# Issuing half of a kernel's input loads from GpSimd instead of SyncE

## The chip, the cores and the metric

The kernel runs on one core of a Trainium2 chip. The metric is device time in microseconds (us); lower is better. Most runs of the kernel before agree within 0.5% (10 of the 11 of the first job lie within 0.5% of their median, 274.85 us). A run is called fast or slow by its distance from the fastest run of the same kernel (over 1.5% is slow). Ratios are computed as the mean time of one kernel's fast runs over that of the other's of the same rounds, so they are not quite the ratio of the medians that are quoted beside them.

TensorE is called PE, VectorE DVE, ScalarE ACT, GpSimd POOL and SyncE SP, as in the profile. PEld is PE's weight load. A name with q (SPq, POOLq) is the engine's sequencer issuing a DMA. The profile counts the DMAs of every engine on the same 16 DMA engines. In it, q1 is SyncE's queue, q10 ACT's (both "hardware_dynamic") and q0 is GpSimd's ("software_dynamic").

## The reference

Linear attention with cosine weights, then an MLP mixer over tokens and channels, eight batches, all in fp32 at the boundary:

```python
# q, k, v: (8 batches, 8 heads, 576 rows, 64); weights: 576x256, 256x576, 512x1536, 1536x512
phi(x) = concat(relu(x) * cos, relu(x) * sin)      # 64 -> 128 features, angle grows with the row
kv  = einsum('bhsf,bhsd->bhfd', phi(k), v);  z = phi(k).sum(rows)
x   = (phi(q) @ kv) / (phi(q) @ z + 1e-6)           # heads joined: (8, 576, 512)
h   = relu(x.T @ w_tok1) @ w_tok2
u   = x + h.T
out = u + relu(u @ w_ch1) @ w_ch2                   # ... cut
```

## The kernel before

It is a pipeline over batches, written as one order of instructions. While PE works on the channel MLP of batch p, it also does the attention and the token MLP of p+1, the features of p+2 are made on ACT and DVE, and the inputs of p+3 are loaded. The first part (batches 0 and 1, and the loads up to batch 4) follows a list of words, PLAN; the rest is a loop over channel blocks with hooks in numbered slots.

Three kinds of DMA matter here. Loads bring q, k and v in rows of 1024 or 1280 bytes. Transposes turn a bf16 tile inside SBUF; `qpT` (features of q) and `uT` (input of the channel MLP) are read by PE as weights and operands. Stores write the result. All of these go out from SyncE, so one queue (q1, 48.77 MB in the page below) holds them, in program order in SyncE's timeline below. GpSimd loads the weights early, and later only casts.

```python
def load(b, t, hs=slice(0, H), eng=nc.sync):          # two DMAs: 512 rows of 1024 B, 512 rows of 1280 B
    ...
    for par in (1 - b % 2, b % 2):
        n, f = count(b % 2, par), row0(b % 2, par)
        dmas.append(eng.dma_start(out=x[par::2, hs, raw_span(b % 2, par)], in_=...))

def ldp(b, t, g, g_="n"):                             # as ld, but issued by GpSimd; unused before
    d = load(b, t, heads(g), nc.gpsimd)
...
    def turnx(self, j, n):                            # qpT: 16 + 16 + 8 blocks of 128x128 a batch
        nc.sync.dma_start_transpose(out=self.sb("qpT")[:, j * H:(j + n) * H, :], in_=self.qp[:, j:j + n]...)
    def ubc(self, g, eng="P"):                        # ub: bf16 cast of u on GpSimd
        copy(eng, self.sb("ub")[:, js, :], self.u[:, js, :])
    def utx(self, g):                                 # uT: two transposes of 256 KB a batch
        nc.sync.dma_start_transpose(out=self.sb("uT")[:, 2*g:2*g+2]..., in_=self.ub[:, 2*g:2*g+2]...)
    def o(self, j):                                   # stores; store_batch does the same in the loop
        ...nc.sync.dma_start(out=out_rows(self.b, p_, j - 1, 2), in_=self.u[p_::2, j - 1:j + 1, :])
...
def hooks_for(n, m, nxt):                             # n = p+1, m = p+2, nxt = p+3; at(slot, function, ...)
    if nxt is not None:
        at(0, load, nxt, "k")
        at(0, load, nxt, "q")
        at(9, load, nxt, "v")
    ...                                               # kv, num (reads qpT), mix, u_all (casts ub, uT)
    if m is not None:
        ...                                           # v casts on GpSimd in slots 3 to 7
        at(12, m.turnx, 0, 2)
        at(15, m.turnx, 2, 2)
        at(16, m.turnx, 4, 1)
```

## Time and profile before

| | before |
|---|---|
| time, median of 3 runs | 275.25 us (274.46 to 275.7) |
| span of the profiled run | 273.6 us |
| PE busy | 262.1 us, 96% |
| PE's waits for transposes | 1.6 us, once |
| channel blocks, start to start | 27.6, 29.3, 27.6, 27.6 us |

The first lines are of the page of the kernel before: the span, each engine's busy time with its share of the span and its instructions; each DMA queue's packets, megabytes and share of the 16 engines' time; and the chain of work that ended last, summed by engine.

```profile
span 273.6 us, 4855 instructions
PE 262.1 (96%) x1923; PEld 137.7 (50%) x1941; DVE 172.1 (63%) x346; ACT 110.9 (41%) x176; POOL 47.6 (17%) x67
...
q1 hardware_dynamic: 74512, 48.77, 66.0%
q0 software_dynamic: 4144, 3.77, 9.1%
...
PE 89%; DMA 5%; DVE 4%; issue 1%; DVEq 0%
```

PE is the bound, and there is little else to gain. The one wait inside the pipeline shows in the same chain, in order of time (start, length, what):

```profile
117.84 5.79 DMA qpT<-qp
...
123.68 0.43 PE nf L390 x8
```

The chain passes through 5.79 us of a qpT transpose, but PE had other work during most of it: it waited 1.6 us. What it costs is read better from the starts of the kv matmuls, one set for each channel block, in PE's timeline (start, length, engine, line, operation):

```profile
89.11 1.44 PE L361 MATMUL kv<-vbf,kp 128*128 128x65 bf16 x40
116.71 1.43 PE L361 MATMUL kv<-vbf,kp 128*128 128x65 bf16 x40
146.04 1.43 PE L361 MATMUL kv<-vbf,kp 128*128 128x65 bf16 x40
```

The distances are 27.60 and 29.33 us, and the next ones are 27.6 us again: the block with the wait is 1.7 us longer. SyncE's timeline shows why the transpose came late (start, length of the issue, sequencer, line, operation):

```profile
83.08 2.63 SPq L472 DMA_TRANSPOSE uT<-ub  x2
...
100.67 4.38 SPq L143 DMA_DIRECT2D vt<-in_v_dram  x2
105.94 6.82 SPq L472 DMA_TRANSPOSE uT<-ub  x2
112.85 1.22 SPq L503 DMA_TRANSPOSE uT_tail<-utb  x1
114.17 1.59 SPq L354 DMA_TRANSPOSE qpT<-qp  x1
```

The uT transposes of 105.94 us stand behind loads that the DMA engines have not finished: the first of the v loads of 100.67 us landed 10.7 us after its issue. The transposes' own issue takes 6.82 us instead of 2.63, and the qpT transposes behind them are late. The uT transposes of 83.08 us, by contrast, had the engines nearly to themselves: all 2268 packets of the stretch were under 512 B. The view of the DMAs between 83 and 86 us gives the queue's packets, megabytes and share of the 16 engines' time, and for each kind of issue its count and median time to landing in us:

```profile
q1 hardware_dynamic: 2268, 0.56, 98.4%
...
uT<-ub SPq DMA_TRANSPOSE x2, 3.2
```

### The profile page before, as it was taken

Reading aid. Unit: us, or ns where it says so; the run is one execution under the profiler, and the core shown is the slowest. Engines: PE = TensorE matmul, PEld = TensorE weight load, DVE = VectorE, ACT = ScalarE, POOL = GpSimd, SP = SyncE. Lnnn points to the kernel's source line nnn. Section 1 sums busy time; section 2 is a strip of 40 time slices with the busy share of each in tenths; the row PEclk is TensorE's granted clock in tenths of the full one; section 3 lists DMA queues with packets and bytes.
Section 4 is the critical chain, followed back from the end, with each engine's and each line's share of the span. In section 5 each row is a group of like instructions: output and inputs, shape, how many; then the busy total and the mean of one; then the engine's idle time right before and its main releaser. Section 6 shows DMA issues by size and latency. Waiting matters only on the chain.

```text
span 273.6 us, 4855 instructions
## 1 busy us (share of the span) xinstructions
PE 262.1 (96%) x1923; PEld 137.7 (50%) x1941; DVE 172.1 (63%) x346; ACT 110.9 (41%) x176; POOL 47.6 (17%) x67
## 2 busy tenths in 40 slices
PE   6988999999999999989999999999999999999994
PEld 2875556465444644454446544554455444444443
DVE  6489798899872658835794769476837643424422
ACT  2885281475590548052903391339133201301300
POOL 2172070040041043400250026002000120000000
PEclk9999999999999999999999999999999999999998
DMA  6999999999999999999999948900980062012012
GB/s 206 360 238 170 287 199 238 365 207 211 378 249 196 330 380 361 206 216 297 340 196 235 352 156 175 230 37 2 219 204 2 0 153 98 0 44 109 2 67 87
DMA packets 79079, 53.37 MB, mean 195 GB/s; under 512 B 47824, under 2 KB 76496, under 8 KB 79056
## 3 DMA queue, kind: packets, MB, share of 16 engines
q1 hardware_dynamic: 74512, 48.77, 66.0%
q0 software_dynamic: 4144, 3.77, 9.1%
q10 hardware_dynamic: 400, 0.52, 0.5%
q8 instruction: 15, 0.25, 0.4%
q14 instruction: 8, 0.07, 0.1%
HBM read 35.85 MB, written 9.44 MB: 166 GB/s over the span
## 4 chain that ended last, share of the span: by engine, by line
PE 89%; DMA 5%; DVE 4%; issue 1%; DVEq 0%
PE o_ps L606 25%; PE c_ps L589 25%; PE c L512 8%; PE o L524 7%; PE b L433 6%; PE u L460 5%; PE kv L361 4%; DMA kt<-in_k_dram 3%; PE nf L390 3%; DMA qpT<-qp 2%; DVE kp L332 1%; PE ut L488 1%; PE tr L345 1%; PE o_ps L598 1%; PE nm L390 1%; DVE x L413 1%
## 5 line engine op out<-in xcount | busy, mean ns | idle before, releaser
L268 ACT ACTIVATE h<-c_ps 128x512 bf16<-128x512 f32 x52 | 31.0, 597 | 109.6 <-PE c_ps L589 66.0
L606 PE MATMUL o_ps<-wc,h 128*128 128x512 bf16 x317 | 71.5, 379 | 0.4
L589 PE MATMUL c_ps<-uT,wc 128*128 128x512 bf16 x288 | 70.4, 379 | 0.0
L606 PEld LDWEIGHTS <-h 128*128 128x128 bf16 x324 | 31.7, 98 | 38.2
L589 PEld LDWEIGHTS <-wc 128*128 128x128 bf16 x336 | 30.8, 98 | 32.6
L270 DVE TENSOR_SCALAR h<-c_ps 128x512 bf16<-128x512 f32 x32 | 22.0, 688 | 28.4 <-PE c_ps L589 28.4
L264 POOL CAST ub<-u 128x1024 bf16<-128x1024 f32 x14 | 14.9, 1066 | 106.4 <-issue 63.2
L330 ACT ACTIVATE qp<-qt,cos_t 128x512 bf16<-128x512 f32 x33 | 23.1, 713 | 13.6 <-DMA qt<-in_q_dram 12.1
L609 DVE TENSOR_TENSOR u<-o_ps,u 128x512 f32<-128x512 f32 x24 | 16.5, 689 | 18.5 <-PE o_ps L606 18.5
L264 POOL CAST vbf<-vt 128x512 bf16<-128x512 f32 (+3 forms) x28 | 19.5, 731 | 49.6 <-DMA vt<-in_v_dram 47.3
L512 PE MATMUL c<-uT,wc 128*128 128x512 bf16 x96 | 22.7, 379 | 0.1
L524 PE MATMUL o<-wc,h 128*128 128x512 bf16 x92 | 21.6, 379 | 0.2
L413 DVE TENSOR_TENSOR x<-nf,den 128x512 bf16<-128x512 f32 x30 | 20.7, 692 | 1.0
L330 ACT ACTIVATE qp<-qt,sin_t 128x512 bf16<-128x512 f32 x30 | 21.1, 712 | 0.0
L390 PEld LDWEIGHTS <-qpT 128*128 128x128 bf16 x320 | 15.2, 98 | 11.6 <-DMA qpT<-qp 2.1
L332 DVE TENSOR_SCALAR kp<-kt,cos_t 128x512 bf16<-128x512 f32 x30 | 17.4, 582 | 5.1 <-DMA kt<-in_k_dram 5.1
L465 DVE TENSOR_TENSOR u<-u,x 128x1024 f32<-128x1024 f32 x16 | 19.4, 1220 | 1.7 <-PE u L460 1.7
L433 PE MATMUL b<-x,w 128*128 128x512 bf16 (+1 forms) x84 | 19.8, 354 | 0.3
L332 DVE TENSOR_SCALAR kp<-kt,sin_t 128x512 bf16<-128x512 f32 x31 | 17.9, 582 | 0.6 <-DMA kt<-in_k_dram 0.6
L409 DVE TENSOR_SCALAR den<-nf 128x8 f32<-128x8 f32 x30 | 5.0, 166 | 17.7 <-PE nf L390 17.7
L460 PE MATMUL u<-B,w 128*128 128x512 bf16 x64 | 16.1, 379 | 0.0
L524 PEld LDWEIGHTS <-h 128*128 128x128 bf16 x96 | 9.1, 98 | 10.2
(92 smaller groups left out, 249.4 us busy)
## 6 DMA issues: line engine op xcount, KB each, us to landing
out_dram<-u SPq DMA_DIRECT2D x32, 256.0 KB, 2.7
qt<-in_q_dram SPq DMA_DIRECT2D x8, 640.0 KB, 7.4
kt<-in_k_dram SPq DMA_DIRECT2D x8, 640.0 KB, 7.8
qt<-in_q_dram SPq DMA_DIRECT2D x8, 512.0 KB, 6.3
kt<-in_k_dram SPq DMA_DIRECT2D x8, 512.0 KB, 6.7
vt<-in_v_dram SPq DMA_DIRECT2D x6, 640.0 KB, 9.9
vt<-in_v_dram SPq DMA_DIRECT2D x6, 512.0 KB, 8.8
wc<-in_moe_w_ch_dram POOLq DMA_DIRECT2D x4, 384.0 KB, 7.7
```

Source lines behind the costliest of these rows:

```text
L264: (nc.scalar.copy if eng == "A" else ENG[eng].tensor_copy)(dst, src)
L268: nc.scalar.activation(dst, src, AF.Relu)
L330: nc.scalar.activation(dst, src, AF.Relu, scale=tab)
L332: ENG[eng].tensor_scalar(dst, src, scalar1=tab, scalar2=0.0, op0=ALU.mult, op1=ALU.max)
L390: nc.tensor.matmul(nm[:, hh * (D + 1):(hh + 1) * (D + 1)], self.qpT[:, j * H + h, :], self.kv[:, h, :D + 1], start=(not eps or hh == 0), s ...
L413: nc.vector.tensor_mul(dst, nmv[:, :, :, :D], den_b)
L433: nc.tensor.matmul(b1[:, mi], w1[:, col(self.c, j), mi * P:(mi + 1) * P], self.x[:, j, cs], start=(j == 0 and (g == 2 or mi == 0)), stop=( ...
L460: nc.tensor.matmul(ps[:, jj], w2[:, ki, 1 + 2 * g + jj, :], self.B1[:, ki, :], start=(ki == 0), stop=(ki == NT - 1))
L512: nc.tensor.matmul(ps, wc1[:, ki, mi * P:(mi + 1) * P], self.uT[:, :, ki, :], start=(ki == 0), stop=(ki == NCC - 1))
L524: nc.tensor.matmul(self.ps["o", j], self.h1[:, ki, j * P:(j + 1) * P], wc2[:, ki, :], start=(ki == 0), stop=(ki == NCH - 1))
L589: nc.tensor.matmul(c_ps, wc1[:, ki, mi * P:(mi + 1) * P], uT[:, :, ki, :], start=(ki == 0), stop=(ki == NCC - 1))
L606: nc.tensor.matmul(o_ps, h1[:, ki, j * P:(j + 1) * P], wc2[:, ki, :], start=(ki == 0), stop=(ki == NCH - 1))
```

## The change

The intent is to take the loads of batches 4 to 7 out of the transposes' queue. Loads go to GpSimd, and SyncE's queue holds only transposes and stores from then on, so that no transpose stands behind a load.

```diff
-utx.2.1 dnj.1.0.0 utx.2.0 ld.4.q.2 dnj.1.2.0 tb.1 ...
-... cast.3.2.1.2.P feat.3.k.2.2.1.D ld.4.v.2.k22 dnj.1.1.0 dnj.1.1.1 ld.4.k.2.k32 ...
+utx.2.1 dnj.1.0.0 utx.2.0 ldp.4.q.2 dnj.1.2.0 tb.1 ...
+... cast.3.2.1.2.P feat.3.k.2.2.1.D ldp.4.v.2.k22 dnj.1.1.0 dnj.1.1.1 ldp.4.k.2.k32 ...
@@ hooks_for
         if nxt is not None:
-            at(0, load, nxt, "k")
-            at(0, load, nxt, "q")
-            at(9, load, nxt, "v")
+            at(0, load, nxt, "k", slice(0, H), nc.gpsimd)
+            at(0, load, nxt, "q", slice(0, H), nc.gpsimd)
+            at(9, load, nxt, "v", slice(0, H), nc.gpsimd)
```

More of the change, by code (lines that the diff above doesn't have):

```diff
@@ L52 @@
 cast.3.1.1.2.P uo.2.1 ubc.2.1 uo.2.0 dnj.1.3.0 dnj.1.3.1 cast.3.3.1.2.D turnx.3.0.2 feat.3.k.0.2.0.A ubc.2.0
-utx.2.1 dnj.1.0.0 utx.2.0 ld.4.q.2 dnj.1.2.0 tb.1 feat.3.k.4.2.0.A dnj.1.2.1 cast.3.0.1.2.D o.1.2
-feat.3.k.1.2.0.A cast.3.2.1.2.P feat.3.k.2.2.1.D ld.4.v.2.k22 dnj.1.1.0 dnj.1.1.1 ld.4.k.2.k32 feat.3.k.3.2.1.A
-dnj.1.0.1 feat.3.k.3.2.0.A feat.3.k.1.2.1.A o.1.0 o.1.3 tm.2 to.2 o.1.1
+utx.2.1 dnj.1.0.0 utx.2.0 ldp.4.q.2 dnj.1.2.0 tb.1 feat.3.k.4.2.0.A dnj.1.2.1 cast.3.0.1.2.D o.1.2
+feat.3.k.1.2.0.A cast.3.2.1.2.P feat.3.k.2.2.1.D ldp.4.v.2.k22 dnj.1.1.0 dnj.1.1.1 ldp.4.k.2.k32
+feat.3.k.3.2.1.A dnj.1.0.1 feat.3.k.3.2.0.A feat.3.k.1.2.1.A o.1.0 o.1.3 tm.2 to.2 o.1.1
 """
```

## The prediction

> **What bounds the kernel now.** TensorE: the page gives PE 262.1 us busy of a 273.6 us span (96%), granted clock near 1.00; the chain of waits is 89% PE, 5% DMA, 4% DVE. Its DMA part is 7.8 us for the first k load (untouched) and one wait of 5.79 us on a transpose of q features (qpT), 117.84 to 123.68 us. That wait costs less than its length: channel blocks start at 88.4, 116.0, 145.3, 172.9, 200.5 us and last 27.6 us, but the one with this wait 29.3 us. So 1.75 us is all that faster transposes can win; elsewhere PE is busy 1.95 to 2.00 of every 2 us (table of windows).
>
> **Why that wait is there.** In the SyncE queue's timeline, loads of batches 4 and 5 are issued from 85.8 to 105 us, at 311 to 393 GB/s. The uT transposes behind them take 3.97 and 2.76 us to issue (1.26 undisturbed) and 7.9 and 5.3 us to land (3.1 to 3.3), and push the qpT transposes from about 110 to 114.2 and 117.8 us.
>
> **What the change moves.** 24 load issues go from SyncE (0.6 to 0.75 us each, more when backed up) to GpSimd, which paid 0.7 to 0.8 us per weight load: 17 to 19 us more on an engine 17% busy. Order on PE, DVE and ACT is the same. GpSimd's queue is in order, so a load's wait for its buffer holds back later casts; I find no harmful case: the k loads wait for the last k feature (115.3 us) with only v casts behind them, due 30 us later, and the ub casts come after loads already issued.
>
> **Where it helps.** [...] Then transposes no longer stand behind whole loads: batch 4's qpT goes out near 110 and 113 us and lands before its use at 122. Gain: 1.75 us, likely the whole.
>
> **Where it hurts.** Loads start as soon as GpSimd is free: q4 near 82.2 instead of 85.8 us, v4 near 85 instead of 88.6, k5 near 88 instead of 95. The uT transposes of batch 2 (issued 83.08 and 84.4, landed near 87.5, first read by PE at 88.4: 0.9 us of slack) had the DMA engines almost alone; now they share them with a stream of loads. If they take 5 to 7 us to land instead of 3.2, PE stalls 1 to 3 us; my estimate is 1.6. Later, k of batches 6 and 7 (near 115 and 145 us) overlaps the last qpT transposes, which have 2 to 5 us of slack: 0.2 us.
>
> **Sum.** 275.25 - 1.75 + 1.6 + 0.2 = about 275.2; predicted 275.2 us, 8 in 10 between 273.2 and 278.2. Faster by over 2%: 0.01; within 2%: 0.94; slower by over 2%: 0.05.
>
> **What the profile would show.** Right: the block near 116 us lasts 27.6 us and its qpT wait is gone; a new PE wait on a uT transpose near 88 us; SyncE issues of uT back to 1.3 us in the next block; 14 MB more on the software queue; GpSimd issues near 0.75 us. Wrong: PE waits for qpT or uT at 145 us or later; ub casts starting later after DVE's u.
>
> **What would make it wrong.** The share that transposes get against loads is unmeasured: if small, several transposes stall PE by 3 us or more each; if large, the stall at 88 us vanishes (273.5). GpSimd issue may take much longer for 512 rows of 1 to 1.25 KB, or block when many loads are outstanding, delaying ub casts.

## The result, and the profile after

| | before | after |
|---|---|---|
| median, first job | 274.86 us (274.15 to 275.7, 4 runs) | 324.02 us (320.94 to 329.42, 4 runs) |
| ratio of fast runs | | 1.1698 [1.1624, 1.1773] |

The kernel became 17% slower. Two of the four runs count as slow by the rule above, the profiled one among them. The changed kernel was therefore run again (the first experiment, below): 327.37 us, ratio 1.1927, with a profile in the fast state. That profile is the one read here. The scatter of about 3% belongs to the changed kernel.

The page of the changed kernel, same lines as before:

```profile
span 323.1 us, 4860 instructions
PE 267.5 (83%) x1923; PEld 139.7 (43%) x1941; DVE 170.0 (53%) x346; ACT 111.0 (34%) x176; POOL 62.9 (19%) x91
...
q1 hardware_dynamic: 61840, 34.61, 44.4%
q0 software_dynamic: 7600, 17.93, 24.2%
...
PE 59%; DMA 30%; DVE 3%; SPq 3%; POOL 2%; issue 1%; ACT 0%; POOLq 0%; DVEq 0%
```

PE is busy 83% of the time and the chain is 30% DMA. PE's waits (engine, line, what for: total, times, longest):

```profile
PE nf L390 <- DMA qpT<-qp: 25.6, 2, 15.5
PE c_ps L589 <- DMA uT<-ub: 20.0, 1, 20.0
```

And their places in PE's timeline, with the wait in brackets:

```profile
109.63 1.87 PE L589 MATMUL c_ps<-uT,wc 128*128 128x512 bf16 x4 [19.98 <-DMA uT<-ub]
160.46 0.62 PE L390 MATMUL nf<-kv,qpT 128*128 128x65 bf16 x8 [15.53 <-DMA qpT<-qp]
202.18 0.62 PE L390 MATMUL nf<-kv,qpT 128*128 128x65 bf16 x8 [10.05 <-DMA qpT<-qp]
```

Three waits on transposes hold nearly the whole loss. The span is 323.1 - 273.6 = 49.5 us longer. The waits are 45.6 us, less the 1.6 us that were there before. PE's busy time is 267.5 - 262.1 = 5.4 us more. That sums to 49.4 us. The extra busy time has a visible source: four matmuls of this shape took 1.87 us at 109.63 us, and 1.03 us at 88.25 us in the kernel before. The table by stretches gives the granted clock there (stretch, its length, busy time of PE, PEld, DVE, ACT and POOL, clock, DMA share, GB/s):

```profile
104.00:106.00 2.00, 0.00 (x0) 0.00 (x0) 0.00 (x0) 0.00 (x0) 0.00 (x0) 0.50 1.05 355
110.00:112.00 2.00, 2.00 (x17) 1.17 (x16) 0.00 (x0) 0.42 (x1) 0.00 (x0) 0.50 1.01 324
```

The clock is at 0.50 while PE idles and still 0.50 in the first 2 us of work after the wait; at 114 us it is back at 1.00. The stretches at 0.50 behind the two qpT waits end at 164.0 and 205.0 us. PE was busy 9.5 us in the three together; if that work takes half the time at a clock of 1.00, as an estimate 4.7 of the 5.4 us come from the clock (the four matmuls above took 1.87 against 1.03 us). Here a long wait is paid a second time.

Now the DMAs. The second of the two uT transposes, issued at 85.65 us, in the view of the DMAs from 86 to 88 us:

```profile
uT<-ub SPq DMA_TRANSPOSE x1, 23.8
```

It took 23.8 us to land instead of 3.2 (the first, issued at 84.27 us, took 10.2). What the engines did meanwhile, from 96 to 106 us (packets, MB, share of the 16 engines' time):

```profile
DMA packets 1646, 3.51 MB, mean 351 GB/s; under 512 B 930, under 2 KB 930, under 8 KB 1645
...
q0 software_dynamic: 804, 3.28, 93.2%
q1 hardware_dynamic: 841, 0.21, 10.6%
```

This is the central reading. The two queues sent almost the same number of packets, 804 and 841. But a packet of the loads holds 4096 or 5120 B (by the record of each packet in the first profile of this kernel), and a packet of the transposes 0.21 MB / 841 = 256 B. Packet for packet, the transposes get one part in ten of the engines' time (10.6%). Nothing is idle in this stretch: the two shares add up to 103.8%, and the engines move 351 GB/s. The transposes, on which PE waits, get 6% of the bytes.

The page itself shows the packets' size. SyncE's queue lost 74512 - 61840 = 12672 packets and GpSimd's gained 7600 - 4144 = 3456, for the same 14.16 MB in 24 loads. That is 528 packets a load from SyncE and 144 from GpSimd. A load has 512 rows: 512 + 16 and 128 + 16, with 16 more packets per load in either case, of 4 B by the same record. SyncE sends one row in a packet, GpSimd four.

The rest of the change did what it was meant to. GpSimd's timeline in that stretch:

```profile
83.35 1.43 POOL L143 DMA_DIRECT2D qt<-in_q_dram  x2
...
86.25 1.38 POOL L143 DMA_DIRECT2D vt<-in_v_dram  x2 [0.30 <-POOL vbf L264]
87.61 2.74 POOL L143 DMA_DIRECT2D kt<-in_k_dram  x4
```

An issue takes about 0.7 us, loads go out earlier than before (v of batch 4 at 86.25 instead of 88.57 us, k of batch 5 by 90 instead of 95), and the uT transposes of the next block, with no loads about, take 2.96 us for two issues, not 6.82.

### The profile page after: what moved, and what is told of

It is laid out like the page before. It is cut to its first block, busy times and chain, and to the rows that moved or that the text cites. A ratio compares the mean times of both kernels' runs of the same rounds, so it can differ in the third digit from the quotient of the medians.

```text
span 327.6 us, 4878 instructions
## 1 busy us (share of the span) xinstructions
PE 269.3 (82%) x1941; PEld 140.2 (43%) x1941; DVE 170.4 (52%) x346; ACT 111.0 (34%) x176; POOL 63.0 (19%) x91
## 3 DMA queue, kind: packets, MB, share of 16 engines
q1 hardware_dynamic: 61840, 34.61, 45.0%
## 4 chain that ended last, share of the span: by engine, by line
PE 65%; DMA 25%; DVE 5%; SPq 2%; POOL 1%; issue 1%; DVEq 0%; POOLq 0%
PE c_ps L589 20%; PE o_ps L606 19%; DMA qpT<-qp 13%; DMA uT<-ub 8%; PE b L433 5%; PE c L512 4%; PE u L460 4%; PE o L524 3%; PE kv L361 3%; DMA kt<-in_k_dram 2%; PE nf L390 2%; DMA out_dram<-u 2%; DVE kp L332 1%; PE tr L345 1%; PE ut L488 1%; SPq L354 1%
## 5 line engine op out<-in xcount | busy, mean ns | idle before, releaser
L589 PE MATMUL c_ps<-uT,wc 128*128 128x512 bf16 x288 | 74.3, 394 | 23.6 <-DMA uT<-ub 23.6
L589 PEld LDWEIGHTS <-wc 128*128 128x128 bf16 x336 | 31.6, 100 | 58.5 <-issue 27.8
L606 PEld LDWEIGHTS <-h 128*128 128x128 bf16 x324 | 31.7, 98 | 38.2
L264 POOL CAST ub<-u 128x1024 bf16<-128x1024 f32 x14 | 14.9, 1068 | 138.1 <-DVE u L465 118.2
L390 PE MATMUL nf<-kv,qpT 128*128 128x65 bf16 x240 | 13.2, 199 | 26.2 <-DMA qpT<-qp 25.8
L330 ACT ACTIVATE qp<-qt,cos_t 128x512 bf16<-128x512 f32 x33 | 23.1, 713 | 15.5 <-DMA qt<-in_q_dram 13.5
L264 POOL CAST vbf<-vt 128x512 bf16<-128x512 f32 (+3 forms) x28 | 18.4, 694 | 40.5 <-DMA vt<-in_v_dram 39.3
L413 DVE TENSOR_TENSOR x<-nf,den 128x512 bf16<-128x512 f32 x30 | 20.7, 692 | 1.0
L433 PE MATMUL b<-x,w 128*128 128x512 bf16 (+1 forms) x90 | 21.2, 368 | 0.0
L332 DVE TENSOR_SCALAR kp<-kt,cos_t 128x512 bf16<-128x512 f32 x30 | 16.4, 549 | 4.7 <-DMA kt<-in_k_dram 4.7
L332 DVE TENSOR_SCALAR kp<-kt,sin_t 128x512 bf16<-128x512 f32 x31 | 16.8, 548 | 0.9 <-DMA kt<-in_k_dram 0.9
```

The lines of the kernel that those rows point to most:

```text
L264: (nc.scalar.copy if eng == "A" else ENG[eng].tensor_copy)(dst, src)
L330: nc.scalar.activation(dst, src, AF.Relu, scale=tab)
L332: ENG[eng].tensor_scalar(dst, src, scalar1=tab, scalar2=0.0, op0=ALU.mult, op1=ALU.max)
L390: nc.tensor.matmul(nm[:, hh * (D + 1):(hh + 1) * (D + 1)], self.qpT[:, j * H + h, :], self.kv[:, h, :D + 1], start=(not eps or hh == 0), s ...
L433: nc.tensor.matmul(b1[:, mi], w1[:, col(self.c, j), mi * P:(mi + 1) * P], self.x[:, j, cs], start=(j == 0 and (g == 2 or mi == 0)), stop=( ...
L589: nc.tensor.matmul(c_ps, wc1[:, ki, mi * P:(mi + 1) * P], uT[:, :, ki, :], start=(ki == 0), stop=(ki == NCC - 1))
```

## The experiments

Theories of why the transposes are slow, conjectures of the author's that the runs tell apart below:

1. Shares: each DMA engine takes a packet from each queue in turn, whatever its size, so what counts is the size of the packets beside the transposes.
2. Switching: mixing two queues, or transposes with copies, costs the DMA engines time, so all traffic slows.
3. Transposes as such are sensitive, and a plain copy of the same packets would not be.
4. GpSimd as such: its queue is favoured, or its load issues hold back its own casts in order, and transposes start late.

Where an expectation uses letters, S1 is the first of these, S2 the second and S3 the first half of the fourth; S alone says only that transposes starve beside GpSimd's loads. Other letters are explained where they stand. The experiments e1 to e4 ran in one job, e5 to e8 in a second, e9 to e11 in a third, and e12 alone; each job had its own runs of the kernel before (medians 274.85, 274.68, 275.38 and 275.51 us). Kernels called wrong give wrong output and are used for their traces.

### e1: the changed kernel again

No edit.

> The changed kernel itself, once more, for a profile in the fast state. Every theory: about 320 to 323 us, PE waits of some 15 to 24 us on a uT transpose near 88 us and on qpT transposes of the next two channel blocks, in a fast run too. If the long waits show only in slow runs, the slow state and not the change makes them.

Measured: 327.37 us (324.93 to 329.31), ratio 1.1927 [1.1866, 1.1988]. The profile is the one read above. The result stands, in a second job and in fast runs alone, though above the 320 to 323 us expected. Theory 4's second half falls here: GpSimd's first ub cast of batch 2 starts 1.9 us after DVE's u (2.0 before), and the first uT transpose is issued at 84.27 us, as soon as SyncE has issued the qpT transposes ahead of it, again as before.

### e2: only batch 4's loads moved

```diff
-            at(0, load, nxt, "k", slice(0, H), nc.gpsimd)
-            at(0, load, nxt, "q", slice(0, H), nc.gpsimd)
-            at(9, load, nxt, "v", slice(0, H), nc.gpsimd)
+            at(0, load, nxt, "k")
+            at(0, load, nxt, "q")
+            at(9, load, nxt, "v")
```

> Only batch 4's loads (the three words of the schedule list) are issued by GpSimd; batches 5 to 7 stay on SyncE. Theory S (transposes starve while GpSimd-issued loads are outstanding): the uT transposes of batch 2 land only when most of 3.5 MB of q4, v4, k4 have been moved, near 97 to 100 us instead of 87.5, so PE stalls about 10 us at 88 us, and later blocks are as before: about 285 us. Rival G (GpSimd's in-order queue delays its casts): ub casts would start late after DVE's u and the loss would not go with transposes; with only 6 loads moved and none of them waiting long, about 276 us.

Measured: 292.01 us (290.17 to 293.21), ratio 1.0612 [1.0565, 1.0659]. PE waits 18.3 us for uT, and for no qpT. The second uT transpose, issued at 83.32 us, took 22.8 us to land. So the first wait comes from moving six load issues alone, and the two qpT waits from the other eighteen. But the wait is nearly twice the 10 us expected of 3.5 MB of loads, and the time is 7 us over; e8 comes back to this.

### e6: only the loads of batches 5 to 7 moved

The reverse of e2: PLAN as before, the three hooks as in the change.

> The other half of the change: batch 4's loads stay on SyncE, those of batches 5 to 7 are issued by GpSimd. Theory S1: the wait of 20 us at 88 us is gone or small (k5 and q5 are issued near 89 us, after the uT transposes), the two later waits on qpT of 10 to 17 us each stay: 298 to 305 us. Together with batch 4's part (292.0) the two losses should add up to about that of the whole change, 17 + 25 to 30 = 42 to 50 us. Rival (one cause early on that shifts everything): the later waits go with the first one, under 285 us.

Measured: 306.15 us median, and only one of four runs counts as fast (299.72; the others 305.41, 306.9, 310.28), so no ratio is given, and the profile is a slow one. It shows two qpT waits, 18.7 us together, and one of 6.7 us on a DVE add that itself waited for a store. Added up, e2 loses 17 us and the fast run of e6 25 us, 42 together, against 46 to 52 for the whole change. The parts nearly add up; the scatter of the runs hides the rest.

### e3: the changed kernel, with q and k loads held back until the transposes have landed

The q load of batch 4 waits for the last uT transpose of batch 2, and the k load of each later block waits for the last qpT transpose of the batch before. All 24 loads stay on GpSimd.

```diff
-utx.2.1 dnj.1.0.0 utx.2.0 ldp.4.q.2 dnj.1.2.0 tb.1 ...
+utx.2.1 dnj.1.0.0 utx.2.0 ldp.4.q.2.uT2 dnj.1.2.0 tb.1 ...
...
+    def gated(b, t, name):
+        gate(load(b, t, slice(0, H), nc.gpsimd)[0], name)      # wait for landed[name]
...
-            at(0, load, nxt, "k", slice(0, H), nc.gpsimd)
+            at(0, gated, nxt, "k", f"qpT{nxt - 2}")
```

> All 24 loads still issued by GpSimd, but batch 4's q waits for the last uT transpose of batch 2 to land, and the k load at the start of each channel block waits for the last qpT transpose of the batch before it, so that few transposes are in flight with these loads. Theory S: the starving goes, 273 to 277 us. Rival G (in-order GpSimd queue): GpSimd waits longer than before, so at least as slow as the changed kernel, 320 us or more. Rival D (GpSimd-issued loads are slow in themselves): still 290 us or more, with PE, ACT or DVE waiting for q, k or v loads.

Measured: 275.47 us (274.71 to 276.33), ratio 1.0022 [0.9993, 1.0051]. The same loads on the same queue, moved in time by a few microseconds, cost nothing: the whole 17 to 19% is the overlap in time with transposes. One wait on a transpose was left:

```profile
125.09 0.43 PE L390 MATMUL nf<-kv,qpT 128*128 128x65 bf16 x8 [2.96 <-DMA qpT<-qp]
```

Here the v load of batch 5, which has no gate, goes out at 102.09 us and meets the uT transposes of 105.92 us.

### e4: the disputed share measured by itself

A small kernel (wrong) in phases. Each phase issues 4.2 MB of loads, then two 512 KB transposes (or plain SBUF copies in 256 B rows) from SyncE. Phases differ in who issues the loads, and in their row length in words of 4 bytes.

```python
def loads(tag, eng, words):        # two loads of 2 MB, rows of `words` fp32, not adjacent in memory
    src = flat.rearrange("(p a f) -> p a f", p=P, f=words * 9 // 8)
    ... eng.dma_start(out=t, in_=src[:, i * n:(i + 1) * n, :words])
PHASES = (("A", None, 0, "t"), ("B", "g", 256, ""), ("C", "g", 256, "t"), ("D", "a", 256, ""), ("E", "a", 256, "t"),
          ("F", "a", 1024, "t"), ("G", "g", 1024, "t"), ("H", None, 0, "c"), ("I", "g", 256, "c"), ("J", "a", 256, "c"),
          ("K", "s", 256, "t"), ("L", "a", 64, "t"))     # g GpSimd, a ACT, s SyncE; t transposes, c copies
```

> A kernel made for measuring (its result is wrong on purpose: it stores zeros). Twelve phases one after the other: A two transposes of 512 KB on SyncE alone; B 4.2 MB of loads in 1 KB rows from GpSimd alone; C B with the transposes; D loads in 1 KB rows from ACT alone; E D with transposes; F ACT loads in 4 KB rows with transposes; G GpSimd loads in 4 KB rows with transposes; H two SBUF-to-SBUF copies of 512 KB in 256 B rows on SyncE alone; I H with GpSimd loads; J H with ACT loads in 1 KB rows; K loads and then transposes, all on SyncE; L ACT loads in 256 B rows with transposes. Theory S1 (engines alternate between queues packet by packet, and GpSimd's packets are 4 KB against 256 B of a transpose): alone the second transpose lands about 7 us after the first issue; C, F and G much the same, last transpose 14 to 20 us; E clearly less (9 to 13), L least; copies I suffer like C. Rival S2 (alternating between transposes and copies costs the engines a switch each time): C, E, F, G and L all slow, L the worst, total throughput well under 350 GB/s in all of them, while I and J keep their throughput. Rival S3 (only GpSimd's descriptor path hurts): C, G and I slow, E, F, J and L near the time alone plus their share.

Measured, from the views of the DMAs in a stretch where both run (packets per us of the transposes or copies = packets over the stretch's length):

| phase | loads | beside them | load packets : SyncE packets | SyncE packets per us |
|---|---|---|---|---|
| A | none | transposes | 0 : 3741 in 5 us | 748 |
| C | GpSimd, rows of 1 KB | transposes | 718 : 921 in 9 us | 102 |
| G | GpSimd, rows of 4 KB | transposes | 821 : 959 in 9 us | 107 |
| F | ACT, rows of 4 KB | transposes | 831 : 991 in 9 us | 110 |
| E | ACT, rows of 1 KB | transposes | 2736 : 2514 in 10 us | 251 |
| L | ACT, rows of 256 B | transposes | 5147 : 4136 in 9 us | 460 |
| I | GpSimd, rows of 1 KB | copies | 669 : 1332 in 9 us | 148 |
| J | ACT, rows of 1 KB | copies | 2338 : 1998 in 9 us | 222 |

The lines of phase F (87 to 96 us), of G (105 to 114 us) and of E (70 to 80 us), in this order:

```profile
q10 hardware_dynamic: 831, 3.27, 90.9%
q1 hardware_dynamic: 991, 0.25, 13.2%
```

```profile
q0 software_dynamic: 821, 3.24, 91.4%
q1 hardware_dynamic: 959, 0.25, 13.9%
```

```profile
q10 hardware_dynamic: 2736, 2.77, 83.5%
q1 hardware_dynamic: 2514, 0.64, 31.2%
```

F and G differ only in the engine that issues the loads, and are alike (110 and 107 packets per us): GpSimd as such is not favoured. F and E differ only in the row length of the loads, and the transposes go 2.3 times as fast in E. C shows GpSimd putting four rows of 1 KB into one packet (2.83 MB / 718 = 3.9 KB), and it behaves like rows of 4 KB (102 packets per us). Copies suffer too (148 packets per us in I, 222 in J), so transposes are not special, though copies got two packets for each of GpSimd's (1332 to 669), not one. The stretches with loads move 319 to 392 GB/s but L, whose packets are all small (262): the engines lose no time by mixing here, so theory 2 falls for this kernel. (In the real one some stretches are much slower, see e8.) The loads in 1 KB rows end nearly when they would: the second of them landed 14 us after its issue alone (B, D) and in 15 to 16 us beside transposes (C, E).

One thing was badly chosen. With so few loads, both streams end within 16 to 20 us in every phase but L (24), and the second transpose's landing after the first one's issue (16.0 us in C, 14.1 in G, 14.4 in E, where 9 to 13 was expected) says little; the packet counts tell.

### e5: the changed kernel with the loads on ACT

```diff
-        d = load(b, t, heads(g), nc.gpsimd)
+        d = load(b, t, heads(g), nc.scalar)
```

The three hooks were changed alike. ACT's queue is a hardware queue, with one row in a packet (1.18 MB in 1058 packets below).

> The same 24 loads at the same places of the program, issued by ACT (hardware queue, packets of one row, 1024 or 1280 B) instead of GpSimd (packets of four rows, 4096 or 5120 B). Theory S1 (one packet each in turn, so the size of the loads' packets sets how long a transpose takes): in the measuring kernel beside 1 KB packets the transposes moved 2514 packets in 10 us, beside 4 KB packets 921 in 9 us, so the same transposes land about 2.5 times sooner here; PE waits of some 5 us at 88 us and 0 to 5 us later, 278 to 290 us. Rival S0 (any queue of their own lets the loads starve the transposes): 315 us or more.

Measured: 285.47 us (284.86 to 286.06), ratio 1.0401 [1.0376, 1.0426]. The uT transposes landed in 5.7 us instead of 23.8, and PE waited 4.0 us for them. In the view of the DMAs from 84 to 92 us:

```profile
q1 hardware_dynamic: 4262, 1.07, 61.2%
q10 hardware_dynamic: 1058, 1.18, 44.8%
...
uT<-ub SPq DMA_TRANSPOSE x2, 5.7
```

This is the same pair of competitors in the real kernel, with the loads' packets about a quarter as large. It isn't a pure test, as ACT's place in program order issues the loads at other times: only v of batch 4 (83.4 us) and part of k (89.4 us) meet these transposes. Nor did any of ACT's load packets take over 1.04 us, where GpSimd's took up to 4.8 (see e8), so packet size may not be the whole difference. No wait for qpT remains. The rest of the 11 us is another price: a pair of load issues holds ACT's own queue for 1.3 to 4.3 us, and PE waits 2.5 us for kv copies and 1.3 us for features that ACT makes late.

### e7: the one load without a gate moved behind the transposes

As e3, and the v loads of batches 5 to 7 go from slot 9 of one channel block to slot 0 of the next, behind the same wait.

```diff
-            at(9, load, nxt, "v", slice(0, H), nc.gpsimd)
...
+        if m is not None and m.b > 4:
+            at(0, gated, m.b, "v", f"qpT{m.b - 1}")
```

> As the gated version, but the v loads of batches 5 to 7 are moved to the start of the next channel block, behind the same wait for qpT, because in the gated version v5 (issued at 102 us) still met the uT transposes (105.9 us) and left a wait of 2.96 us. Theory S1: that wait goes; all blocks last 27.6 us and the time is 272.5 to 273.6 us, 0.5 to 0.9% under the kernel before. If it stays at 275, the wait there has another cause.

Measured: 274.41 us (273.63 to 274.68), ratio 0.9986 [0.9969, 1.0002]. The expected 272.5 to 273.6 us was missed. The qpT wait went away and its block took 27.65 us. But the gated q load of batch 4 stood ahead of a v cast in GpSimd's queue until 88.1 us (the text of e9 has 87.0), and PE waited 0.8 us for the kv matmul of that cast. This is an in-order loss, of the kind the prediction looked for; the gate caused it, not the change.

### e9: the gated q load behind the casts

```diff
-... utx.2.0 ldp.4.q.2.uT2 dnj.1.2.0 tb.1 ...
-... cast.3.2.1.2.P feat.3.k.2.2.1.D ldp.4.v.2.k22 ...
+... utx.2.0 dnj.1.2.0 tb.1 ...
+... cast.3.2.1.2.P feat.3.k.2.2.1.D ldp.4.q.2.uT2 ldp.4.v.2.k22 ...
```

> As the second gated version, but the gated load of batch 4's q stands behind the two casts that it held back there (GpSimd waited at it until 87.0 us, so one v cast of batch 3 came at 88.97 us and PE's kv matmuls of that block waited 0.83 us; the block lasted 28.6 instead of 27.6 us). If GpSimd's in-order wait is what ate the gain, the block is back to 27.6 us and the time is 272.9 to 273.5 us, ratio 0.994 to 0.996. If not, 274.4 again.

Measured: 273.78 us (273.02 to 274.32), ratio 0.9935 [0.9899, 0.9971]. PE waits for no transpose. The time is 0.3 us above the range expected. The gain of the prediction's "Where it helps" exists: some 1.6 us by the medians of the job, once no load is beside a transpose.

### e10: the kernel before, with the v loads later, all on SyncE

Is GpSimd's queue needed for that gain? This edit is to the kernel before.

```diff
-            at(9, load, nxt, "v")
...
+        if m is not None and m.b > 4:
+            at(0, load, m.b, "v")
```

> The kernel before with all loads on SyncE, but the v loads of batches 5 to 7 issued at the start of the next channel block, behind the qpT transposes, as in the gated versions. If the 1.75 us wait of the kernel before comes from the order of loads and transposes and not from sharing one queue, the wait on qpT in the block at 116 us goes here as well: 272.8 to 273.6 us, the same as the gated version, and GpSimd's queue gives nothing. If a shared queue is what costs, it stays near 274.7.

Measured: 273.65 us (273.19 to 274.53), ratio 0.9928 [0.9889, 0.9966], as e9 within its interval and at the edge of the range expected. kv starts are 90.35, 117.94, 145.52, 173.10 and 200.69 us: every block 27.6 us. In SyncE's timeline the v load now follows the last qpT transposes:

```profile
107.36 3.69 SPq L472 DMA_TRANSPOSE uT<-ub  x2
...
116.20 4.34 SPq L354 DMA_TRANSPOSE qpT<-qp  x2
...
122.64 1.38 SPq L143 DMA_DIRECT2D vt<-in_v_dram  x2
```

A second queue gains nothing over a better order in one. Both kernels are about 0.7% faster than the kernel before, far below 2%.

### e8: turn-taking with the kernel's own loads

The waits for qpT were longer than the turns seemed to explain, so this small kernel (wrong) takes the kernel's exact load pattern: 64 partitions with 8 rows of 1024 B, then 64 with 8 rows of 1280 B, for k, q and v.

```python
(("M", "g", "k", ""), ("N", "g", "k", "after"), ("O", "a", "k", "after"), ("Q", "g", "k", "before"),
 ("R", "a", "k", "before"), ("S", "g", "kk", "after"), ("T", "g", "k", "copy"))   # kk: 7 MB; before: transposes issued first
```

> A second measuring kernel (result wrong on purpose). Loads as the kernel has them (64 partitions, 8 runs of 1024 B, then 64 others with 8 of 1280 B; k, q, v of a batch, 3.5 MB): M from GpSimd alone; N with two transposes of 512 KB issued about 3 us after them; O as N from ACT; Q GpSimd, transposes issued 2 us before the loads; R as Q from ACT; S as N with 7 MB of loads; T GpSimd with 256 B SBUF copies in place of transposes. Theory S1: in N, Q, S and T about one packet of the loads per packet of the other queue, all transposes landing only as the loads run out (S: 20 us or more); in O and R sooner. Besides, in the changed kernel some load packets took 1 to 5 us and the engines moved only 36 to 120 GB/s for 5 us, which the first measuring kernel did not show: if this comes from the shape of the loads it appears in N and S, if from transposes already under way it appears in Q (and R) only, if from neither it appears nowhere.

Measured: the transposes landed 12.3 to 12.4 us after issue beside 3.5 MB from GpSimd (N), 7.1 and 11.7 beside ACT's (O), and 21.6 to 21.7 beside 7 MB from GpSimd (S). In Q and R the transposes, issued ahead of the loads, landed in 4.3 to 8.3 us, where for Q a landing only as the loads run out was expected; copies beside GpSimd's loads (T) took 12.3 and 13.2 us. In S, from 103 to 116 us:

```profile
q0 software_dynamic: 1068, 4.35, 94.4%
q1 hardware_dynamic: 1067, 0.27, 9.9%
```

In this stretch, one for one. That gives a way to reckon the wait. The uT transposes are 512 KB, 2048 packets of 256 B, 128 for each of 16 engines if they are spread evenly. In the changed kernel an engine sent one every 16 x 10 us / 841 = 0.19 us between 96 and 106 us. As an estimate, 128 x 0.19 = 24 us, against the measured 23.8. The closeness is partly luck: the rate is taken from the same wait, and it was not even (some 880 packets of SyncE's queue went from 90 to 92 us). S is the independent measure: 21.6 us beside 7 MB, where the changed kernel moved 6.74 MB of GpSimd's loads from 84 to 110 us. So turn-taking explains most of the first wait in e1.

It does not explain the others, nor that of e2. There the uT transposes met the 3.5 MB of batch 4 alone, as in N, where twice as many bytes of transposes landed in 12.3 to 12.4 us; they took 22.8 us. The view of the DMAs from 88 to 96 us in e2:

```profile
DMA packets 1138, 1.10 MB, mean 138 GB/s; under 512 B 941, under 2 KB 941, under 8 KB 1138
...
q0 software_dynamic: 217, 0.88, 72.7%
q1 hardware_dynamic: 921, 0.23, 45.7%
```

A load packet took 0.43 us in the mean (72.7% of 16 x 8 us over 217), up to 3.5 us by the trace's record of each packet, and a transposing packet 0.06 us, where alone (83 to 86 us before) it took 0.02. So traffic of both queues slowed. As an estimate, turns explain 12.4 of these 22.8 us; the other 10.4 are more than half of PE's wait of 18.3 us.

The qpT transposes issued from 137 us in the changed kernel landed up to 23.0 us later, again beside only as many loads as in N. The view of the DMAs from 144 to 149 us shows the same:

```profile
DMA packets 175, 0.37 MB, mean 75 GB/s; under 512 B 106, under 2 KB 106, under 8 KB 174
...
q0 software_dynamic: 72, 0.33, 85.3%
q1 hardware_dynamic: 102, 0.03, 22.5%
```

Here 72 load packets took 85.3% of 16 engines x 5 us, 0.95 us each, where a 5120 B packet beside transposes took about 0.23 us in e8 (from the trace's record of each packet). The longest took 4.79 us. No packet in e8 took over 1.6 us, so e8 doesn't show this second cause.

### e11: what makes single load packets slow

Another small kernel (wrong): the kernel's load pattern and transposes, with and without stores ahead in SyncE's queue, GpSimd's casts, and a busy PE and ACT.

```python
PHASES = (("U", "g", "st"), ("V", "g", "t"), ("W", "g", "stc"), ("X", "g", "stcb"), ("Y", "a", "st"))
# g GpSimd, a ACT; s stores, t transposes, c casts, b busy PE and ACT
```

> A third measuring kernel (result wrong on purpose), to find what makes packets of GpSimd's loads take 2 to 5 us in the changed kernel. Loads of one batch as the kernel has them with one transpose of 512 KB and one of 256 KB: U two stores of 256 KB ahead of the transposes on SyncE, loads from GpSimd at the same time; V the same without the stores; W as U with five casts on GpSimd between the q and the v loads; X as W with PE and ACT kept busy; Y as U with the loads from ACT. If the stores among them bring the slow packets, U, W, X show packets over 2 us and the transposes land 20 us or more after issue, V 10 to 12; if GpSimd's casts or busy engines bring them, only W and X, or X. If none shows packets over 2 us, the cause stays open.

Measured, with the packets' times from the trace's record of each packet: the 512 KB transpose landed 17.7 us after issue in U, 14.2 in V, 20.7 in W, 17.4 in X and 13.5 in Y. The longest load packet took 2.24 us in U, 1.17 in V, 2.79 in W, 3.08 in X and 0.89 in Y. Stores go with longer packets (U against V), but each phase is one look at one time, and none reaches 4.79 us. Nor were stores moving at the time: the longest packets of U, W and X began at 17.0, 56.1 and 78.8 us, and the last packet of a store had ended by 14.9, 53.1 and 76.7 us. V landed later than the 10 to 12 us expected, U and X sooner than 20.

### e12: the changed kernel with the stores cut

The stores of batches 1 to 3 keep their place in the queue but write one row of 4 KB (wrong).

```diff
-                    nc.sync.dma_start(out=out_rows(b, par, j - 1, 2), in_=u[par::2, j - 1:j + 1, :])
+                    e_ = par + 2 if b in (1, 2, 3) else P
+                    nc.sync.dma_start(out=out_rows(b, par, j - 1, 2)[:(e_ - par + 1) // 2], in_=u[par:e_:2, j - 1:j + 1, :])
```

> The changed kernel with the stores of batches 1, 2 and 3 cut to one row of 4 KB each (128 KB to 256 KB less each; those parts of the output are missing on purpose), in the same places of SyncE's queue with the same waits. In the measuring kernels the stores ahead of the transposes went with load packets of 2 to 3 us (only in the phases with stores) and with 3.5 to 6.5 us more until the transpose landed. If the stores make the slow packets, the waits of 15.5 and 10 us on qpT fall to about 6 and 3 us, the wait of 20 us on uT stays near 17 (packets in turn alone: 21.6 us to land beside 7 MB), and the time is 298 to 310 us. If slow packets of 2 to 5 us and waits of 15 and 10 us are still there, 318 us or more, and the stores are not what makes them in the kernel.

Measured: 310.27 us median (301.79 to 313.63); only the run of 301.79 us counts as fast, and the profile (311.9 us span) is slow. Its waits are 23.0 us for uT and 10.8 us for qpT, the latter 25.6 us in e1. Load packets of up to 3.2 us still appear, and 57 took over 2 us, against 47 in e1. So shorter qpT waits went with cutting the stores, on a single slow profile, but the slow packets stayed. In e2 no store was moving at all beside them: from 83 to 96 us every packet of SyncE's queue had 256 B or 4 B, and load packets took up to 3.5 us. Stores are therefore not needed for it. What slows single load packets stays open.

## Why the prediction was wrong

Point by point, in its own order:

- "TensorE bounds", and "1.75 us is all that faster transposes can win": right. Without overlap (e9) and with a better order (e10) the kernel gained 0.65% and 0.72%, 1.6 and 1.7 us by the medians of that job.
- "Why that wait is there": right. e10 moves one load behind the transposes and all blocks take 27.6 us.
- "What the change moves": right. 24 issues of about 0.7 us, 14.16 MB more on the software queue, earlier loads, and no harmful case of in-order blocking in the changed kernel. That GpSimd's queue holds casts back in order shows in e7: a v cast stood behind the gated load until 88.1 us.
- "Where it helps" saw in two queues a reason for help alone. In the traces the DMA engines sent about as many packets of one queue as of the other, 804 of the loads against 841, and 1068 against 1067 in e8. The wait that it was to remove grew instead: it is the same wait, 5.4 us after the start of the second block's kv matmuls, that ends at 160.46 us in e1 and is 15.5 us long. The transposes no longer stood behind loads of the same queue (two uT issues took 2.96 us), but beside those of batch 6. Without any such overlap the gain does come (e9, e10).
- "Where it hurts" is the step that failed. It named the right transposes, the right place and the right cause, the engines' time shared with loads, and mis-sized the term: "If they take 5 to 7 us to land instead of 3.2, PE stalls 1 to 3 us; my estimate is 1.6". The second of them took 23.8 us in e1 and 27.4 in the first profile, and PE stalled 20.0 and 23.6 us. The second half of the same step, "k of batches 6 and 7 ... overlaps the last qpT transposes, which have 2 to 5 us of slack: 0.2 us", measured 15.5 + 10.1 us. Together the two terms were 1.8 us on record and 45.6 us on the chip. A further 5.4 us of busy time, most of it from the lower granted clock after each wait, were in no term.
- Why the size was off: the estimate of 5 to 7 us was not worked out from packets. Where the queues send about as many packets each (804 and 841 in e1, 1068 and 1067 in e8), the packets' size decides. With such turns, which the trace of before does not show, its numbers give: 128 transposing packets an engine, and a load packet of one row took about 60 ns (16 x 9 us over 2399 packets from 96 to 105 us; by the trace's record of each packet 49 ns for 1024 B and 59 for 1280 B). Had GpSimd's packets been of one row too, as an estimate, 128 x (60 + 20) ns is some 10 us, already above the range (20 ns is a transposing packet alone, 98.4% of 16 x 3 us over 2268). They hold four rows, 4096 B and 5120 B in the trace of the changed kernel, and e4 shows that this factor matters: 102 transposing packets per us beside GpSimd's 1 KB rows, 251 beside ACT's. The trace of before could not tell it: GpSimd's weight loads there averaged 3.77 MB / 4144 = 0.9 KB a packet. Even turns beside packets of four rows, 12.3 us in N, leave about half of e2's 22.8 us open: that part could not have been reckoned from anything on record.
- "What the profile would show": of the signs named as right, a wait on uT, SyncE's quick issues of uT in the next block, 14.16 MB more on the software queue and about 0.7 us an issue on GpSimd came; the block with the qpT wait did not shrink to 27.6 us, it lasted 45.0 us (kv starts of 139.53 and 184.49 us). Of the signs named as wrong, PE waits for qpT after 145 us came (15.5 and 10.1 us); later ub casts did not.
- "What would make it wrong" did name the risk: "The share that transposes get against loads is unmeasured: if small, several transposes stall PE by 3 us or more each". It gave that 0.05. An unmeasured quantity on which the whole sign depends deserved a wider range. The other risk that it named, GpSimd issues that take much longer or block, did not come: about 0.7 us an issue in e1.

Shown by experiment: that overlap in time is the cause (e3, ratio 1.0022), that packet size and not the issuing engine sets the share where the engines move 340 to 392 GB/s (e4: 110 transposing packets per us in F, 107 in G, 251 in E), that the queue itself is worth nothing (ratio 0.9928 without it in e10, 0.9935 with it in e9). Not settled: why single load packets of GpSimd's took 1 to 5 us beside transposes in the kernel (up to 3.5 us in e2, 4.8 us in e1) and the engines moved as little as 75 GB/s there. This made the two qpT waits of e1 and the wait of e2 longer than turns explain. Mixing as such (theory 2) or something of GpSimd's own (theory 4) is therefore not excluded for this part: no load packet took over 1.6 us in e4 and e8 and over 3.1 us in e11, and ACT's took at most 1.07 us in all runs. Stores are not needed for it (e2, e12).

## What to carry to other kernels

Here, moving a bulk transfer to another queue did not get it out of the way; it let the transfer compete with the one that PE waits for, which landed in 23.8 us instead of 3.2. Before doing so, as an estimate, count the packets of the transfer that is waited for, per DMA engine, and multiply by the time of one competing packet (in e1 128 x 0.19 us = 24 us): in e1 and e4 large packets starved small ones while the bandwidth looked perfect (351 GB/s in e1; 387 GB/s in phase G, with 107 transposing packets per us against 748 alone). The estimate can be low: in e2 the landing took 22.8 us, where turns explain 12.4. Where a small transfer is critical, order the bulk behind it (in one queue that is one line moved, worth 1.7 us in e10) and check in the trace that the two don't overlap.
